# Memory attention and two Strassen MoE layers on one core: phi's relu and the gate's arithmetic move to POOL, and the order of the work is sought anew

## The chip, the cores and the metric

One Trainium2 chip, one of its cores. The time is that of one execution on the device, in microseconds (us); the median of several executions is given, and the range they span. Engines: PE is TensorE, DVE is VectorE, ACT is ScalarE, POOL is GpSimd, and SP issues nearly all DMAs.

## What is computed

```python
def _attn_ref(q, k, v, M_prev, z_prev, beta):      # B, H, S, D = 4, 8, 576, 64
    scores = scale * np.matmul(q, k.transpose(0, 1, 3, 2))   # causal mask, then softmax a
    local = np.matmul(a, v)
    def phi(x):
        return np.where(x > 0, x, np.exp(x) - 1.0) + 1.0
    q_p = phi(q)
    mem_ret = np.einsum('bhsd,bhde->bhse', q_p, M_prev)
    mem_norm = np.einsum('bhsd,bhd->bhs', q_p, z_prev)[..., None] + 1e-06
    mem_out = mem_ret / mem_norm
    g = 1.0 / (1.0 + np.exp(-beta))[None, :, None, None]
    return (g * mem_out + (1 - g) * local)

x = attn_out.transpose(0, 2, 1, 3).reshape(2304, 512)
h = x @ w_in; x = (h * tanh(softplus(h))) @ w_out      # first MoE layer, 512 -> 2048 -> 512
h = x @ w_in; x = (h * sigmoid(h)) @ w_out             # second MoE layer, the same sizes
```

## The kernel before, in words

The program is two stages that overlap a little. **Attention** works on 16 pairs of heads (4 batches x 4 pairs). For each pair, PE computes the scores in blocks of queries (steps `s40`, `s41`, `s3`, `s2`, `s1`, `s0`; L595 and L634), DVE evicts each block from PSUM with the mask added and the row's minimum taken (steps `r..`, L588, into a ring of four `sm` buffers), ACT takes the exponential with a row sum (steps `e..`, L615), PE transposes the probabilities (L486), ACT and DVE copy these out of PSUM (L476, L479), and PE multiplies by the values (L692). DVE scales the result into `xT` (L696).

Beside that runs phi of the queries, as a chain of small steps per pair on a 128x576 tile. Before, this chain is: `phu`, u = relu(nq) on ACT (L507); `phn`, e = nq - u on POOL (L505), which is min(nq, 0); `phe`, exp(e) on ACT (L506); `phf`, e + u on POOL (L508), which is phi(q); `phz` and `phy`, products with z on POOL (L509, L512); `phr`, the sum over a head on DVE (L513); `phg`, two small operations on POOL (L516, L517); `phd`, a reciprocal on DVE (L519); `phq`, a 128x8 product on DVE (L520); and the products that go into the probability tiles, on POOL (L534, L539). The softmax sums take the steps `za` (POOL, L641), `zd` (DVE, L643), `zg` and `n00` (POOL, L644 and L647).

The **gate** is computed once, on 128x8 tiles: exp(-beta) on ACT (L434), five operations on DVE (L437 to L441: 1 + exp, its reciprocal, 1 - g, a lower bound, a product), and five small copies on ACT (L446 to L452). Three steps of the first pair wait for it.

**The MoE layers** run on 32 visits (2 layers, 4 groups of the hidden width, 4 blocks of tokens), with 2 x 2 Strassen products in split single precision: L1000 to L1002 are a product's three matmuls, L1068 the second matmul of the layer, L1031 to L1041 the evictions and activations, L1089 the accumulation into `xT`. The weights arrive as raw 64-bit pairs and are decoded on DVE (L806 to L821; the first eight jobs begin on ACT, L804, and have their subtractions on POOL, L842 to L869, beside attention). L964 and L971 split the attention's result for the first products.

The order is not the program's text. Each step is put into a table with its engine, a duration, the steps it depends on and a due time; `plan` simulates the engines, takes on each free engine the ready step with the earliest latest start, and the instructions are issued in that order. A step's latest start is shifted by the numbers of `SHIFT`, a long table that a search has found. Each engine then runs its own list strictly in order, so an instruction whose input is late holds everything behind it on that engine. The functions `plan`, `pair_steps`, `gates`, `steps` and the `register` methods hold all that the change touches.

## Time and profile before

| | before |
|---|---|
| median of 3 runs | 951.5 us |
| lowest and highest run | 950.07 and 951.98 us |
| span of the profiled execution, first to last instruction | 949.0 us |
| PE busy | 921.2 us (97%) |
| DVE busy | 662.5 us (70%) |
| ACT busy | 498.9 us (53%) |
| POOL busy | 140.4 us (15%) |

Of the profiled execution the span is given; the three runs are timed by themselves and stand 1.1 to 3.0 us above it. The busy shares are means over both stages. Attention takes roughly the first 185 us of the span and all of POOL's work; from there on PE is the engine to look at. A row of groups reads: line, engine, operation, output<-inputs, shapes, count | busy us, mean ns of one | idle time of the engine before them and what ended it.

### The profile page before, as it was taken

The numbers are of one execution on the slowest core, as the hardware profiler recorded it, in microseconds if no ns is written. First come the engines' busy times: TensorE is split into PE (matmuls) and PEld (weight loads), VectorE is DVE, ScalarE is ACT, GpSimd is POOL, SyncE is SP. The second block draws the span as 40 slices with busy tenths as digits, with TensorE's granted clock in tenths as the row PEclk, the third lists the DMA queues.
The fourth block names the chain that finished last, engine by engine and source line by source line (L and its number), as shares of the span: only waits on it lengthen the run. The fifth ranks groups of instructions, "written<-read, shape, count | busy, mean of one in ns | idle before, by whom it ended". The sixth has DMA issues, their size and how long they took to land.

```text
span 949.0 us, 17264 instructions
## 1 busy us (share of the span) xinstructions
PE 921.2 (97%) x6544; PEld 813.1 (86%) x6544; DVE 662.5 (70%) x1504; ACT 498.9 (53%) x1172; POOL 140.4 (15%) x223
## 2 busy tenths in 40 slices
PE   4989999999999999999999999999999999999998
PEld 2656666799999999999999999998999888989986
DVE  4899899988984558665957889766647765754333
ACT  5998899876654243433433647554533442433330
POOL 5688798300000000000000000000000000000000
PEclk9999999999999999999999999999999999999999
DMA  6546563666647403850375535704550374024412
GB/s 209 149 158 194 165 199 121 213 261 235 221 150 250 156 1 98 274 156 1 117 253 197 221 119 198 278 23 162 189 177 10 108 265 145 1 93 147 157 54 99
DMA packets 60034, 147.72 MB, mean 156 GB/s; under 512 B 7600, under 2 KB 25136, under 8 KB 59952
## 3 DMA queue, kind: packets, MB, share of 16 engines
q1 hardware_dynamic: 59808, 146.30, 45.4%
q8 instruction: 51, 0.84, 0.4%
q10 hardware_dynamic: 144, 0.33, 0.1%
q14 instruction: 31, 0.25, 0.1%
HBM read 108.79 MB, written 37.81 MB: 154 GB/s over the span
## 4 chain that ended last, share of the span: by engine, by line
PE 85%; DVE 4%; ACT 3%; POOL 3%; issue 2%; DMA 2%; SPq 0%; DVEq 0%; POOLq 0%
PE acc L1068 42%; PE psX L1000 7%; PE psX L1001 7%; PE psX L1002 7%; PE psY L1000 4%; PE psY L1001 4%; PE psY L1002 4%; DVE sm L588 2%; PE psW L1001 2%; PE psW L1002 2%; PE psW L1000 2%; PE ps_t L692 2%; PE ps_s L595 2%; PE ps_t L486 1%; ACT Ph L615 1%
## 5 line engine op out<-in xcount | busy, mean ns | idle before, releaser
L1068 PE MATMUL acc<-g,w 128*128 128x320 f32 (+1 forms) x1152 | 218.3, 337 | 0.0
L1068 PE MATMUL acc<-w,g 128*128 128x512 f32 x864 | 214.4, 394 | 0.0
L1068 PEld LDWEIGHTS acc<-g,w 128*128 128x128 f32 x1152 | 183.8, 188 | 13.1
L1068 PEld LDWEIGHTS acc<-w,g 128*128 128x128 f32 x864 | 157.8, 188 | 30.5
L1031 ACT COPY vt<-psX 128x256 f32<-128x256 f32 (+1 forms) x192 | 75.2, 398 | 154.8 <-PE psX L1002 146.0
L1089 DVE TENSOR_TENSOR xT<-acc,xT 128x512 f32<-128x512 f32 (+1 forms) x126 | 77.2, 613 | 93.8 <-PE acc L1068 92.9
L1041 DVE TENSOR_TENSOR g<-vt,g 128x512 fp32r<-128x512 f32 (+1 forms) x128 | 94.1, 754 | 35.4 <-ACT g L1040 34.7
L1029 DVE TENSOR_TENSOR vt<-psY,vt 128x256 f32<-128x256 f32 (+1 forms) x128 | 57.9, 456 | 87.1 <-ACT vt L1031 46.2
L1040 ACT CAST g<-vt 128x512 fp32r<-128x512 f32 (+1 forms) x128 | 83.4, 672 | 31.5 <-PE acc L1068 30.1
L1000 PE MATMUL psX<-x,w 128*128 128x320 f32 (+1 forms) x256 | 75.8, 296 | 0.0
L1001 PE MATMUL psX<-x,w 128*128 128x320 f32 (+1 forms) x256 | 75.7, 296 | 0.0
L1002 PE MATMUL psX<-x,w 128*128 128x320 f32 (+1 forms) x256 | 75.6, 295 | 0.0
L595 PE MATMUL ps_s<-kT,qT 64*128 64x288 f32 (+3 forms) x320 | 66.8, 480 | 6.3 <-DMA kT<-in_kT_dram 4.6
L1037 ACT ACTIVATE vt<-vt 128x640 f32<-128x640 f32 (+1 forms) x64 | 43.8, 685 | 51.8 <-DVE vt L1029 51.5
L588 DVE CUSTOM_DVE_ANT_0 sm<-ps_s,mask 128x288 f32<-128x288 f32 (+3 forms) x128 | 56.9, 472 | 5.4 <-PE ps_s L595 3.1
L1035 ACT ACTIVATE vt<-vt 128x256 f32<-128x256 f32 (+1 forms) x64 | 28.5, 445 | 59.7 <-DVE vt L1029 59.7
L1036 ACT ACTIVATE vt<-psX 128x256 f32<-128x256 f32 (+1 forms) x64 | 26.0, 407 | 50.2 <-PE psX L1002 50.1
L1029 DVE TENSOR_TENSOR vt<-psW,vt 128x256 f32<-128x256 f32 (+1 forms) x64 | 29.1, 455 | 31.7 <-PE psW L1002 31.2
L1000 PEld LDWEIGHTS psX<-x,w 128*128 128x128 f32 x256 | 48.2, 188 | 2.0 <-issue 0.2
L1001 PEld LDWEIGHTS psX<-x,w 128*128 128x128 f32 x256 | 48.3, 189 | 1.7
L875 ACT CAST w<-val 128x512 fp32r<-128x512 f32 (+1 forms) x64 | 34.8, 567 | 26.5 <-DVE val L866 13.1
L1002 PEld LDWEIGHTS psX<-x,w 128*128 128x128 f32 x256 | 48.3, 188 | 0.0
(126 smaller groups left out, 2019.1 us busy)
## 6 DMA issues: line engine op xcount, KB each, us to landing
stg<-in_moe_w_in_dram SPq DMA_DIRECT2D x32, 512.0 KB, 5.6
stg<-in_moe_w_out_dram SPq DMA_DIRECT2D x32, 512.0 KB, 3.5
x<-sp SPq DMA_DIRECT2D x18, 640.0 KB, 4.2
x<-sp SPq DMA_DIRECT2D x18, 512.0 KB
sp<-x SPq DMA_DIRECT2D x12, 640.0 KB, 2.9
sp<-x SPq DMA_DIRECT2D x12, 512.0 KB, 4.1
nv<-in_v_dram SPq DMA_DIRECT2D x16, 320.0 KB, 4.3
x1T<-sp01T SPq DMA_DIRECT2D x8, 640.0 KB
```

What stands on the lines that cost most here:

```text
L588: nc.vector.tensor_tensor_reduce(out, ps, mask, -0.125, init, ALU.add, ALU.min, acc)
L595: nc.tensor.matmul(ps, lhsT=s["qT"][R[j], qcols(i)], rhs=s["kT"][R[j], k0 + cols.start:k0 + cols.stop], start=True, stop=True)
L1000: nc.tensor.matmul(o, lhsT=W(0, kc), rhs=X(0, kc), start=(n in (1, 2, 7) and kc == 0), stop=False, skip_group_check=True)
L1001: nc.tensor.matmul(o, lhsT=W(0, kc), rhs=X(1, kc), start=False, stop=False, skip_group_check=True)
L1002: nc.tensor.matmul(o, lhsT=W(1, kc), rhs=X(0, kc), start=False, stop=(kc == 1), skip_group_check=True)
L1029: nc.vector.tensor_tensor(o, self.bank[q, to], o, op=ALU.add)
L1031: f[f"s{n}"] = lambda n=n: nc.scalar.copy(val(*at[n]), self.bank[q, "X"])
L1037: f["m2"] = lambda: nc.scalar.activation(val(1), val(1), fn)
L1040: f[f"h{c}"] = lambda c=c: nc.scalar.copy(hi(c), val(c))
L1041: f[f"l{c}"] = lambda c=c: nc.vector.tensor_tensor(self.gt(q, c)[:, 1, :2 * tb], val(c), hi(c).bitcast(F32), op=ALU.subtract)
L1068: nc.tensor.matmul(y, lhsT=a, rhs=b, start=(c == 0 and k == 0), stop=(c == 1 and k == 5))
L1089: nc.vector.tensor_tensor(part, acc, part, op=ALU.add)
```

## The change

It makes five edits. (1) `phu` and `phn` become two independent one-input instructions on POOL: u = max(nq, 0) and e = min(nq, 0); ACT's relu goes. (2) Four of the five gate operations on DVE go to POOL, in two steps `one` and `rest` around the reciprocal `sig`, which stays on DVE. (3) The plan gains a `lock`: a DVE step in that set (`phq`, the weights' bit operations, the splits) is lengthened by what remains of a running POOL step, and a POOL step by what remains of such a DVE step. (4) Durations of the plan are set anew. (5) The table `SHIFT` is another one.

```diff
@@ plan @@
+        port = {"D": 0.0, "G": 0.0}
...
+                    if e == "D" and k in self.lock:
+                        d += max(0.0, port["G"] - now)
+                        port["D"] = now + d
+                    if e == "G":
+                        d += max(0.0, port["D"] - now)
+                        port["G"] = now + d
@@ pair_steps @@
-    E("phu", "A", 0.58, ["ldnq"])
-    E("phn", "G", 1.37, ["phu"])
+    E("phn", "G", 0.9, ["ldnq"])
     E("phe", "A", 0.58, ["phn"])
+    E("phu", "G", 0.9, ["ldnq"])
     E("phf", "G", 1.37, ["phe", "phu"])
@@ gates @@
+        def one():
+            nc.gpsimd.tensor_scalar(bt, bt, 1.0, None, op0=ALU.add)
+
         def sig():
-            nc.vector.tensor_scalar(bt, bt, 1.0, None, op0=ALU.add)
             nc.vector.reciprocal(self.g, bt)
-            nc.vector.tensor_scalar(self.g1, self.g, -1.0, 1.0, op0=ALU.mult, op1=ALU.add)
-            nc.vector.tensor_scalar(self.g1c, self.g1, 1e-20, None, op0=ALU.max)
-            nc.vector.tensor_tensor(self.btg, self.g1c, bt, op=ALU.mult)
+
+        def rest():
+            nc.gpsimd.tensor_scalar(self.g1, self.g, -1.0, 1.0, op0=ALU.mult, op1=ALU.add)
+            nc.gpsimd.tensor_scalar(self.g1c, self.g1, 1e-20, None, op0=ALU.max)
+            nc.gpsimd.tensor_tensor(self.btg, self.g1c, bt, op=ALU.mult)
@@ steps @@
-        f["phn"] = lambda: nc.gpsimd.tensor_tensor(self.get(p, "e"), s["nq"], s["u"], op=ALU.subtract)
+        f["phn"] = lambda: nc.gpsimd.tensor_scalar(self.get(p, "e"), s["nq"], 0.0, None, op0=ALU.min)
         f["phe"] = lambda: nc.scalar.activation(s["e"], s["e"], AF.Exp)
-        f["phu"] = lambda: nc.scalar.activation(self.get(p, "u"), s["nq"], AF.Relu)
+        f["phu"] = lambda: nc.gpsimd.tensor_scalar(self.get(p, "u"), s["nq"], 0.0, None, op0=ALU.max)
@@ register of the attention, of the weights, of the MoE @@
+                if n == "phq":
+                    m.lock.add((p, n))
-            slow = 0.05 if first else 0.0
-            for x, e, d, deps in (("ld", "S", 2.2, []), ("abs", "A", 0.53, ["ld"]) if first else ("abs", "D", 0.465, ["ld"]),
-                                  ("b0", "D", 0.465, ["abs"]), ("b1", "D", 0.465, ["b0"]), ("b2", "D", 0.735, ["b1"]),
-                                  ("b3", "D", 0.735, ["b2"])):
+            for x, e, d, deps in (("ld", "S", 2.2, []), ("abs", "A", 0.57, ["ld"]) if first else ("abs", "D", 0.335, ["ld"]),
+                                  ("b0", "D", 0.335, ["abs"]), ("b1", "D", 0.335, ["b0"]), ("b2", "D", 0.6, ["b1"]),
+                                  ("b3", "D", 0.6, ["b2"])):
+                if e == "D":
+                    m.lock.add(J(x))
-                d2 = lambda n: 0.25 + n / 480 if g == "G" else dve(n)
+                d2 = lambda n: 0.18 + n / 480 if g == "G" else dve(n)
+                m.lock.update(K(x) for x in ["l" + x for x in XOPS] + ["T1", "T2", "T3", "T4"])
-                act2 = lambda n, ps: (0.17 if ps else 0.212) + n / 1200
+                act2 = lambda n, ps: (0.067 if ps else 0.108) + n / 1200
@@ module @@
 def ps2(n):
-    return 0.126 + n / 960
+    return 0.07 + n / 960
 SHIFT = {
-    ('gate', 'exp'): -1546.35, ('gate', 'sig'): -1000.81, ('gate', 'spread'): -1110.7, ('a', 'ldkT'): -1506.04,
...
+    ('gate', 'exp'): -3248.83, ('gate', 'one'): 2030.47, ('gate', 'sig'): 4627.81, ('gate', 'rest'): 1314.36,
...
```

What that does to the lists is seen at three places. Lines shift by 8 to 17 in the changed file: its L600 is L588 of before, L627 is L615, L607 is L595, L517 to L521 are phi's L505 to L509.

The first is the start of DVE's list. L588 (L600) evicts scores; L437 to L441 and L448 are the gate. Before:

```order
L409 MEMSET warm 128x1
L437 TENSOR_SCALAR bt_102<-bt_102 128x8
L438 RECIPROCAL g<-bt_102 128x8
L439 TENSOR_SCALAR g_104<-g 128x8
L440 TENSOR_SCALAR g1c<-g_104 128x8
L441 TENSOR_TENSOR btg<-g1c,bt_102 128x8
L588 ISA sm,m_157<-ps_s,mask 128x288
L588 ISA m_157 128x1
```

Now:

```order
L417 MEMSET warm 128x1
L600 ISA sm,m_149<-ps_s,mask 128x288
L600 ISA m_149 128x1
L600 ISA sm,m_149<-ps_s,mask 128x288
L600 ISA m_149 128x1
L600 ISA sm,m_149<-ps_s,mask,m_149 128x288
L600 ISA m_149 128x1
L600 ISA sm,m_163<-ps_s,smask 128x64
L600 ISA m_163 128x1
L600 ISA sm,m_149<-ps_s,mask,m_149 128x288
L600 ISA m_149 128x1
L448 RECIPROCAL g<-bt_102 128x8
```

The first pair's five score evictions stood behind the whole gate; now they stand ahead of its one remaining DVE operation.

The second is the start of POOL's list, behind the constants. Before:

```order
L505 TENSOR_TENSOR e<-nq,u 128x576 x2
L508 TENSOR_TENSOR e<-e,u 128x576 x2
L509 TENSOR_TENSOR u<-e,z 128x512
L512 TENSOR_TENSOR u<-e,y 128x64
L509 TENSOR_TENSOR u<-e,z 128x512
```

Now:

```order
L519 TENSOR_SCALAR u<-nq 128x576 x2
L517 TENSOR_SCALAR e<-nq 128x576 x2
L445 TENSOR_SCALAR bt_102<-bt_102 128x8
L520 TENSOR_TENSOR e<-e,u 128x576
L451 TENSOR_SCALAR g_104<-g 128x8
L452 TENSOR_SCALAR g1c<-g_104 128x8
L453 TENSOR_TENSOR btg<-g1c,bt_102 128x8
L521 TENSOR_TENSOR u<-e,z 128x512
```

Both relus stand first, so the first pair's minimum is behind the relu of the second pair's queries, and the gate's sum is behind all four.

The third is POOL's list in the middle of attention. Before:

```order
L508 TENSOR_TENSOR e<-e,u 128x576
L505 TENSOR_TENSOR e<-nq,u 128x576
L509 TENSOR_TENSOR u<-e,z 128x512
L512 TENSOR_TENSOR u<-e,y 128x64
L516 TENSOR_SCALAR c<-c 128x9
L517 TENSOR_TENSOR c<-c,bt_108 128x9
L508 TENSOR_TENSOR e<-e,u 128x576
```

Now:

```order
L520 TENSOR_TENSOR e<-e,u 128x576
L517 TENSOR_SCALAR e<-nq 128x576
L521 TENSOR_TENSOR u<-e,z 128x512
L524 TENSOR_TENSOR u<-e,y 128x64
L520 TENSOR_TENSOR e<-e,u 128x576
L528 TENSOR_SCALAR c<-c 128x9
L529 TENSOR_TENSOR c<-c,bt_108 128x9
L519 TENSOR_SCALAR u<-nq 128x576
```

Each pair has one long POOL row more, the relu, and the plan puts it right behind the small operations on `c`.

Elsewhere the lists keep their make-up: up to its last attention instruction each list holds the same attention work but for the moved rows (ACT 16 relus fewer, POOL 20 instructions more), 18 MoE matmuls on PE as before, and the last 48 matmuls before the final group's own are in the same sequence.

## Rows read from the trace of the kernel before

**Rows 1.** Busy time by stretch: us, busy of each engine (instructions), granted clock, DMA, GB/s.

```profile
0.00:15.00 15.00, 2.78 (x14) 1.68 (x16) 4.03 (x11) 4.43 (x12) 6.60 (x14) 1.00 0.76 263
15.00:50.00 35.00, 32.23 (x335) 21.62 (x337) 30.72 (x121) 32.67 (x101) 23.92 (x41) 1.00 0.51 156
50.00:80.00 30.00, 26.40 (x309) 17.34 (x307) 26.22 (x88) 26.05 (x82) 26.46 (x40) 0.96 0.54 168
80.00:110.00 30.00, 29.03 (x318) 19.22 (x318) 26.87 (x96) 26.78 (x82) 22.88 (x37) 0.93 0.57 178
110.00:140.00 30.00, 28.35 (x359) 19.58 (x357) 28.66 (x99) 28.93 (x88) 27.91 (x41) 1.00 0.54 166
140.00:170.00 30.00, 28.28 (x348) 19.21 (x350) 28.54 (x107) 29.34 (x92) 25.65 (x43) 1.00 0.44 137
...
500.00:700.00 200.00, 200.00 (x1224) 183.91 (x1223) 150.72 (x285) 103.09 (x205) 0.00 (x0) 1.00 0.51 182
```

**Rows 2.** Waits of the whole span: engine, line, who ended it: us, times, longest.

```profile
DVE bt L437 <- ACT bt L434: 10.0, 1, 10.0
PE ps_s L634 <- DVE m L588: 7.8, 2, 7.6
```

**Rows 3.** Timeline of the first 24 us: start, length, instruction [idle before, what ended it].

```profile
4.65 2.29 PE L595 MATMUL ps_s<-kT,qT 64*128 64x288 f32 x8 [4.65 <-DMA kT<-in_kT_dram]
...
10.08 0.68 ACT L507 ACTIVATE u<-nq 128x576 f32<-128x576 f32 x1 [3.25 <-DMA nq<-in_q_dram]
...
13.98 0.46 DVE L588 CUSTOM_DVE_ANT_0 sm<-ps_s,mask 128x288 f32<-128x288 f32 x1
...
15.89 0.78 ACT L615 ACTIVATE Ph<-sm,m 128x576 f32<-128x576 f32 x1
...
17.33 0.62 DVE L588 CUSTOM_DVE_ANT_0 sm<-ps_s,mask 128x448 f32<-128x448 f32 x1 [1.33 <-PE ps_s L595]
...
19.56 1.12 PE L486 MATMUL ps_t<-ident,Ph 64*128 64x64 f32 x28
...
23.98 0.78 ACT L615 ACTIVATE Ph<-sm,m 128x576 f32<-128x576 f32 x1
```

**Rows 4.** Groups of POOL's instructions, in the first 186 us.

```profile
L505 POOL TENSOR_TENSOR e<-nq,u 128x576 f32<-128x576 f32 x16 | 22.8, 1422 | 6.5 <-ACT u L507 6.2
...
L647 POOL TENSOR_SCALAR P<-P,r,g1s 128x128 f32<-128x128 f32 x16 | 8.5, 529 | 4.0 <-DVE c L520 3.8 <-DVE r L643 0.3
...
L641 POOL TENSOR_SCALAR z<-z 128x9 f32<-128x9 f32 x16 | 3.9, 245 | 2.8 <-ACT Pl L615 1.7
...
L420 POOL TENSOR_SCALAR_AFFINE_SELECT smask<-smask 64x64 f32<-64x64 f32 x2 | 0.5, 234 | 0.1
...
L413 POOL TENSOR_SCALAR_AFFINE_SELECT mask<-mask 128x128 f32<-128x128 f32 x1 | 0.3, 292 | 0.1
```

**Rows 5.** ACT's group of relus, whole span.

```profile
L507 ACT ACTIVATE u<-nq 128x576 f32<-128x576 f32 x16 | 10.9, 678 | 7.6 <-DMA nq<-in_q_dram 7.2 <-DVE c L513 0.3
```

**Rows 6.** Chain that ended last: the relu's first and last piece after 15 us.

```profile
22.49 0.58 ACT u L507
...
137.37 0.23 ACT u L507
```

**Rows 7.** The same chain: one piece of phn.

```profile
162.26 1.38 POOL e L505
```

**Rows 8.** Line L520 alone: count, duration ns min/median/max, first and last start.

```profile
L520 DVE TENSOR_TENSOR c<-c,z x16: 101/298/1201, 24.3 to 174.8; 128x8 f32<-128x8 f32 x16
```

**Rows 9.** Line L814 alone, up to 186 us and after it.

```profile
L814 DVE TENSOR_SCALAR val<-val x8: 419/688/1328, 34.9 to 180.6; 128x512 f32<-128x512 f32 x8
...
L814 DVE TENSOR_SCALAR val<-val x56: 416/420/1521, 194.6 to 827.2; 128x512 f32<-128x512 f32 x56
```

**Rows 10.** Stretches of 5 us with a lower granted clock, columns as in rows 1.

```profile
75.00:80.00 5.00, 3.56 (x42) 2.51 (x43) 3.89 (x13) 3.18 (x10) 4.12 (x7) 0.75 0.74 239
...
105.00:110.00 5.00, 5.00 (x46) 3.09 (x45) 4.04 (x14) 4.21 (x13) 4.49 (x9) 0.68 0.90 278
```

More of the change, by code (lines that the diff above doesn't have):

```diff
@@ L50, in __init__ @@
         self.mode = {}
+        self.lock = set()
     def add(self, name, eng, dur, deps, fn, due, after=0.0, lag=0.0, cols=None):
@@ L452, in spread @@
                 nc.scalar.copy(self.g1s[r, :], gv[r, j, :])
-        return exp, sig, spread
+        return exp, one, sig, rest, spread
     def load(self, p, nm, queue=None):
@@ L511, in steps @@
             self.bt[b]["z"][:, h0:h0 + 2, :].unsqueeze(1).to_broadcast([P, 4, 2, D]), op=ALU.mult)
-        f["phy"] = lambda: nc.gpsimd.tensor_tensor(s["u"][:, 8], s["e"][:, 8], self.bt[b]["y"][:, hp], op=ALU.mult)
+        f["phy"] = lambda: nc.gpsimd.tensor_tensor(self.get(p, "u")[:, 8], s["e"][:, 8], self.bt[b]["y"][:, hp], op=ALU.mult)
         f["phr"] = lambda: nc.vector.tensor_reduce(out=self.get(p, "c"), in_=s["u"], axis=AX.X, op=ALU.add)
@@ L707, in register @@
         m.cap.update({"A." + r: t[4] for r, t in self.TILES.items()})
-        exp, sig, spread = self.gates()
+        exp, one, sig, rest, spread = self.gates()
         m.add(("gate", "exp"), "A", 0.2, [], exp, 25.0, 5.2)
-        m.add(("gate", "sig"), "D", 1.0, [("gate", "exp")], sig, 26.0)
-        m.add(("gate", "spread"), "A", 1.0, [("gate", "sig")], spread, 28.0)
+        m.add(("gate", "one"), "G", 0.2, [("gate", "exp")], one, 25.5)
+        m.add(("gate", "sig"), "D", 0.12, [("gate", "one")], sig, 26.0)
+        m.add(("gate", "rest"), "G", 0.6, [("gate", "sig")], rest, 27.0)
+        m.add(("gate", "spread"), "A", 0.75, [("gate", "rest")], spread, 28.0)
         for p in range(B * NP):
@@ L886, in register @@
             first = self.first(job)
-            slow = 0.05 if first else 0.0
-            for x, e, d, deps in (("ld", "S", 2.2, []), ("abs", "A", 0.53, ["ld"]) if first else ("abs", "D", 0.465, ["ld"]),
-                                  ("b0", "D", 0.465, ["abs"]), ("b1", "D", 0.465, ["b0"]), ("b2", "D", 0.735, ["b1"]),
-                                  ("b3", "D", 0.735, ["b2"])):
-                m.add(J(x), e, d + (slow if e == "D" else 0.0), [J(y) for y in deps], f[x], t,
+            for x, e, d, deps in (("ld", "S", 2.2, []), ("abs", "A", 0.57, ["ld"]) if first else ("abs", "D", 0.335, ["ld"]),
[3 more added lines that the diff above has]
+                    m.lock.add(J(x))
+                m.add(J(x), e, d, [J(y) for y in deps], f[x], t,
                       lag=1.6 if x == "ld" else 0.0, after=20.0 + 20.0 * n if first and x == "ld" else 0.0)
@@ L1250 @@
 SHIFT = {
-    ('gate', 'exp'): -1546.35, ('gate', 'sig'): -1000.81, ('gate', 'spread'): -1110.7, ('a', 'ldkT'): -1506.04,
[100 rows of a table removed]
+    ('gate', 'exp'): -3248.83, ('gate', 'one'): 2030.47, ('gate', 'sig'): 4627.81, ('gate', 'rest'): 1314.36,
+    ('gate', 'spread'): -895.27, ('a', 'ldkT'): -4376.92, ('ap', 0): -6657.88, ('a', 'ldqT'): -7408.66,
[93 rows of a table added]
 }
```

193 rows, old and new, of the table SHIFT are left out of this document.

## The prediction

> **What bounds the kernel now.** I read the busy time by stretch first [rows 1]. From the end of attention to the last matmul PE is busy in every microsecond: 200.00 of 200.00 us in the stretch that stands for them. Nothing on DVE, ACT or POOL can shorten that part, and the change removes no matmul. POOL works in attention alone. So the whole gain must come from the first 185 us, and the question is where PE waits there. In 15 to 170 us PE is busy 144.3 of 155 us, DVE 141.0, ACT 143.8 and POOL 126.8 (sums of five rows of [rows 1]): 93, 91, 93 and 82%. No engine is the bound by itself; work passes from one to the other, and each engine's list is strictly in order. In the first 15 us PE is busy for 2.78 us only.
>
> The waits say why [rows 2]. DVE waited 10.0 us for the gate's exponential, in front of L437, and PE waited 7.6 us in one piece for a score eviction. The timeline shows the rest [rows 3]. PE finished the first eight score matmuls at 6.94 (4.65 + 2.29). DVE evicted the first of them at 13.98 only, because the gate's five operations stood ahead of it in its list, and the gate's exponential stood on ACT behind a relu that waited for the second pair's queries, which landed just ahead of 10.08. The first softmax exponential ran at 15.89, the first transposes at 19.56.
>
> **The change, part by part.** The sum is made against the profiled span of 949.0 us; the median of the runs stands 2.5 us above it, and the same 2.5 are added at the end.
>
> *The gate and the head of the lists.* DVE's first evictions no longer have the gate ahead of them, so they can start when PE delivers, some 8 us before 13.98. That does not come through whole, since ACT's next piece is `phe` of the first pair, and on POOL the minimum that it needs is behind the second pair's relu. That relu starts when the queries land, at about 10.05. With 0.8 us for a one-input operation (below), relu ends at 10.85, the minimum at 11.65, `phe`, as wide as the relu and taken at its 0.68 [rows 5], at about 12.35, and the first softmax exponential starts there: 3.5 us before 15.89. The block that DVE evicts behind the gate's reciprocal follows POOL's `one`, about 12.6 with both minima, so it starts at 12.9 where it started at 17.33: 4.4 us. From the first exponential to the first transposes it took 3.67 us (19.56 - 15.89); now ACT's list has the second `phe`, the gate's five small copies and one narrow exponential more in between and waits less for DVE, an estimated 1.0 us more, so the transposes start at about 17.0, 2.5 us earlier. From there to the next pair's first exponential it took 4.42 us (23.98 - 19.56); two relus of 0.58 leave that stretch and one narrow exponential of about their half comes in, so this one starts at about 20.8, 3.2 us earlier. I take **-3.0 us**; the bounds are -2.5 and -4.4.
>
> *ACT's relus.* 16 instructions, 10.9 us of ACT [rows 5], of which two lie in the head. What they are worth is read from the chain that ended last: behind 15 us it holds five pieces of relu, four of 0.57 to 0.59 us and one of 0.23 [rows 6], together 2.54. The others lay beside work of other engines. I take **-2.5**; the bounds are 0, if the next wait is as long, and -8.1 (14 of them by 0.58), if ACT were the bound.
>
> *POOL's two for one.* A two-input pass over 576 elements takes 1422 ns [rows 4]. No one-input pass of that size is in the trace. The row nearest in its operands is the affine select: one input, no tensor of scalars, 234 ns at 64 columns and 292 at 128, so 0.91 ns an element and 0.70 us at 576. The row nearest in its name is L647, 529 ns at 128 columns, against 245 for 9 columns of L641: 2.39 ns an element and 1.60 us at 576; but it does two operations an element, with two scalars from tensors. Between 0.70 and 1.60 I take 0.8, close to the affine select, whose operands are those of relu and minimum. POOL then gets 16 x (2 x 0.8 - 1.42) = 2.9 us more, beside 28.2 idle in 15 to 170 (155 - 126.8). The chain holds three pieces of `phn`, 1.37 to 1.38 each [rows 7]; the relu can now run ahead whenever the queries are there, so at best each piece falls to 0.8 (-1.7), at worst both stand in it (+0.7). I take the dearer end, **+0.5**, since the plan puts the relu in the middle of POOL's list, behind `phg`, where it delays the next item.
>
> *The lock.* L520, an 8-column product, took 101 ns at its fastest, 298 in the median and 1201 at its slowest [rows 8]; L814 took 688 in the median beside attention and 420 behind it [rows 9]. DVE stands still then while POOL works: 16 x 0.197 and 8 x 0.268 are 5.3 us. The change does not remove that; it lets the plan see it. POOL is busy 82% of the time and gets more work, so I take **0**, between -2.6 (half avoided) and +0.5. The Trainium skill, "SBUF — State Buffer", section "Who interferes with whom", has a rule that speaks against this edit: the pair of ports that DVE and GpSimd share is held for a whole instruction by whichever began first, the other blocks, and ACT waits on no one. By that rule each relu taken from ACT adds to the time in which DVE can be blocked, and the sum would be 0.1 us worse (2.9 us more POOL on 140.4, of 5.3 us of stalls); the rows of L520 bear it out that the wait reaches a whole POOL instruction.
>
> *The new order.* In MoE PE has no idle time to win. A late eviction or weight would cost PE its whole length; I take 0, since DVE and ACT are busy 150.7 and 103.1 of 200 us there [rows 1]. The tail keeps its sequence of matmuls: 0.
>
> The sum is -3.0 - 2.5 + 0.5 = -5.0, a span of 944.0 and a time of **946.5 us**. A measurement of this kernel can tell about 0.2%, 1.9 us, from no change.
>
> **The rivals.** *More than that.* PE's idle time in 15 to 170 us is 10.7 us (155 - 144.3), and the granted clock was 0.75 in 75 to 80 us, where PE was busy for 3.56 of 5 only, and 0.68 in 105 to 110 [rows 10]: parts of these stretches ran at 1.2 GHz and the rest at 2.4, which lost 5 x 0.25 + 5 x 0.32 = 2.9 us. An order that is fitted better could win half of these 13.6 beside the head: 951.5 - 3.0 - 6.8 = 941.7. For it: the plan of before priced DVE's weight operations without the wait that the rows show. Against: four engines above 80% leave little to reorder.
>
> *No change.* The head's 3 us are lost again at the next late transfer or full ring, since all lists behind it are new: 951.5, within 1.9. Then the edit about the lock would not do what it says either: the order is planned around the lock, but the chip's POOL and DVE meet elsewhere, and L520's median stays at 298.
>
> *POOL becomes the bound, slower.* If relu and minimum cost L647's rate, 1.60 us each, POOL gets 16 x 1.78 = 28.5 us more, 24.9 of them in 14 pairs behind 15 us, where it had 28.2 idle. It would be 98% busy, which its waits for ACT and DVE do not allow. If 10 us of these waits stay, attention grows by about 7; the head gains 1.9 only (two operations of 0.8 us more ahead of `phe`); 951.5 + 7 - 1.9 = 956.6. It decides from about 1.36 us an operation, where 18 us are added. The Trainium skill, "GPSIMD Engine Reference", section "Elementwise — side-by-side cycle accounting", gives 2.6 cycles an element for two inputs and 1.03 for a light body; by the second figure and the 1.2 GHz that it states, 576 elements are an estimated 0.49 us beside the start, and the sum would be 1 us better than mine; by the first, 1.25 us, it would come near this rival.
>
> *A stall in MoE, slower.* One eviction or weight load late by 3 to 6 us on a PE without slack takes the gain back: about 951 to 955. Against: before, PE did not wait there at all.
>
> **How the numbers follow.** The forecast has 0.55 (times of 943 to 949.5), the better order 0.12 (937 to 943), no change 0.16, POOL as the bound 0.12, a stall in MoE 0.05. Faster by over 0.2% are the first two, 0.67; the same 0.16; slower 0.17. The range must leave out no more than 0.2: 940 to 954 holds the forecast, no change, half of the better order and a third of the slower cases, 0.83.
>
> **What would show it.** Right: the first eviction on DVE starts before 7 us and the first transposes near 17; no relu on ACT; the two one-input rows at 0.7 to 0.9 us; POOL's busy time near 144 us (140.4 + 2.9 + four small rows of the gate); PE without idle time from the end of attention on; PE reaching the first second-layer matmuls 4 to 6 us earlier. Wrong: one-input rows above 1.3 us with POOL over 95% busy, a new long wait of PE or a lower clock between 20 and 180 us, or any idle time of PE in MoE.

## The result and the profile after

The changed kernel takes 957.8 us in the median (955.9 to 959.6), the kernel before 951.7 in the runs beside it: the ratio is 1.0066, with a 95% interval of 1.0046 to 1.0085. It is slower by 6 us, where 946.5 was forecast, and the time lies outside the range. The time is that of the rival "POOL becomes the bound, slower" (956.6), in part by luck, as told below.

The page of the changed kernel:

```profile
span 955.5 us, 17182 instructions
...
PE 923.2 (97%) x6544; PEld 813.3 (85%) x6544; DVE 652.9 (68%) x1500; ACT 494.5 (52%) x1156; POOL 170.1 (18%) x243
...
PE 87%; POOL 6%; DVE 3%; issue 1%; DMA 1%; SPq 1%; ACT 1%; DVEq 0%; POOLq 0%; ACTq 0%
```

POOL's busy time was 140.4 us and is 170.1; the forecast said 144. The last row is the chain that ended last, by engine: POOL has 6% of it, before 3%. Of the 6.5 us that the span is longer, PE's busy time has 2.0 (921.2 to 923.2) and PE's idle time 4.5. All of it lies in attention: POOL's last row that goes into the probability tiles starts at 183.39 us, before at 176.50.

Busy time by stretch, columns as in [rows 1]:

```profile
0.00:15.00 15.00, 5.60 (x20) 3.79 (x20) 1.92 (x11) 3.32 (x7) 9.01 (x16) 1.00 0.66 220
15.00:170.00 155.00, 138.75 (x1602) 92.90 (x1602) 136.88 (x485) 132.69 (x414) 146.10 (x206) 0.98 0.54 163
110.00:140.00 30.00, 26.44 (x295) 17.00 (x297) 26.20 (x92) 25.09 (x76) 29.05 (x42) 0.94 0.54 176
140.00:170.00 30.00, 28.30 (x336) 19.28 (x332) 27.41 (x90) 24.85 (x77) 28.52 (x39) 0.95 0.52 149
500.00:700.00 200.00, 200.00 (x1244) 185.00 (x1243) 151.05 (x293) 103.75 (x211) 0.00 (x0) 1.00 0.51 183
```

In 15 to 170 us POOL is busy 146.1 of 155 us (94%; before 126.8, [rows 1]), and the other three engines all do less there than before: PE 138.8 (144.3), DVE 136.9 (141.0), ACT 132.7 (143.8). One engine rose and the others wait for it, so that less of attention is done in this stretch. PE's idle time fell by 2.8 us in the first 15 (12.2 to 9.4) and rose by 5.5 in the next 155 (10.7 to 16.2). MoE is as full as before.

POOL's groups, first 200 us; the first and the last answer to L505 and L647 of [rows 4]:

```profile
L517 POOL TENSOR_SCALAR e<-nq 128x576 f32<-128x576 f32 x16 | 27.5, 1723 | 0.3
L519 POOL TENSOR_SCALAR u<-nq 128x576 f32<-128x576 f32 x16 | 27.2, 1700 | 5.2 <-DMA nq<-in_q_dram 5.2
L520 POOL TENSOR_TENSOR e<-e,u 128x576 f32<-128x576 f32 x16 | 22.9, 1434 | 1.3 <-ACT e L518 1.2
...
L659 POOL TENSOR_SCALAR P<-P,r,g1s 128x128 f32<-128x128 f32 x16 | 7.2, 448 | 2.6 <-DVE r L655 1.4 <-DVE c L532 1.2
```

The minimum and the relu take 1.72 and 1.70 us each, not 0.8. A pass with one input and a constant is dearer here than the sum of two tensors of the same size (L520, 1.43). 54.7 us stand where 22.8 stood: 31.9 more, with 29.7 net on POOL.

Waits of the first 200 us, columns as in [rows 2]:

```profile
ACT e L518 <- POOL e L517: 14.6, 9, 8.0
...
PEld ps_t L577 <- POOL rx L656: 8.9, 9, 1.6
...
DVE g L448 <- POOL bt L445: 6.2, 1, 6.2
PE ps_s L646 <- DVE m L600: 6.2, 3, 5.0
```

The two waits of [rows 2] had DVE behind ACT and PE behind DVE. Now ACT's exponential waits for POOL's minimum, PE's transposes of the sums wait for POOL's `rx`, DVE's reciprocal for POOL's gate sum. PE's wait for DVE's score evictions is still there, 6.2 us in place of 7.8.

The head, columns as in [rows 3]:

```profile
6.42 1.66 POOL L519 TENSOR_SCALAR u<-nq 128x576 f32<-128x576 f32 x1 [3.20 <-DMA nq<-in_q_dram]
7.15 0.46 DVE L600 CUSTOM_DVE_ANT_0 sm<-ps_s,mask 128x288 f32<-128x288 f32 x1 [6.30 <-PE ps_s L607]
...
10.08 1.64 POOL L519 TENSOR_SCALAR u<-nq 128x576 f32<-128x576 f32 x1 [2.00 <-DMA nq<-in_q_dram]
11.69 3.26 POOL L517 TENSOR_SCALAR e<-nq 128x576 f32<-128x576 f32 x2
13.37 0.68 ACT L518 ACTIVATE e<-e 128x576 f32<-128x576 f32 x1 [8.00 <-POOL e L517]
13.96 0.76 ACT L627 ACTIVATE Ph<-sm,m 128x576 f32<-128x576 f32 x1
...
15.20 0.20 DVE L448 RECIPROCAL g<-bt 128x8 f32<-128x8 f32 x1 [6.18 <-POOL bt L445]
...
19.41 1.76 PE L498 MATMUL ps_t<-ident,Ph 64*128 64x64 f32 x28 [0.85 <-ACT Ph L627]
```

DVE's first eviction starts at 7.15, where it was 13.98. The chain behind it is the one that the prediction followed, relu at 10.08, minimum, `phe`, first softmax exponential, but in steps of 1.65 us in place of 0.8: the exponential is at 13.96 where 12.35 was forecast, and the first transposes are at 19.41, 0.15 us ahead of before.

### The profile page after: what moved, and what is told of

It is laid out like the page before. It is cut to its first block, busy times and chain, and to the rows that moved or that the text cites. A ratio compares the mean times of both kernels' runs of the same rounds, so it can differ in the third digit from the quotient of the medians.

```text
span 955.5 us, 17182 instructions
## 1 busy us (share of the span) xinstructions
PE 923.2 (97%) x6544; PEld 813.3 (85%) x6544; DVE 652.9 (68%) x1500; ACT 494.5 (52%) x1156; POOL 170.1 (18%) x243
## 4 chain that ended last, share of the span: by engine, by line
PE 87%; POOL 6%; DVE 3%; issue 1%; DMA 1%; SPq 1%; ACT 1%; DVEq 0%; POOLq 0%; ACTq 0%
PE acc L1085 42%; PE psX L1017 7%; PE psX L1018 7%; PE psX L1019 7%; PE psY L1017 4%; PE psY L1018 4%; PE psY L1019 4%; PE ps_t L704 3%; PE ps_s L607 2%; PE psW L1017 2%; PE psW L1018 2%; PE psW L1019 2%; PE ps_t L498 2%; POOL e L517 1%; DVE sm L600 1%
## 5 line engine op out<-in xcount | busy, mean ns | idle before, releaser
L1085 PE MATMUL acc<-g,w 128*128 128x320 f32 (+1 forms) x1152 | 213.2, 337 | 0.0
L1057 ACT CAST g<-vt 128x640 fp32r<-128x640 f32 (+1 forms) x128 | 82.3, 673 | 92.3 <-PE acc L1085 91.1
L1017 PE MATMUL psX<-x,w 128*128 128x256 f32 (+1 forms) x256 | 75.7, 296 | 0.0
L1018 PE MATMUL psX<-x,w 128*128 128x256 f32 (+1 forms) x256 | 75.7, 296 | 0.0
L1019 PE MATMUL psX<-x,w 128*128 128x256 f32 (+1 forms) x256 | 75.6, 295 | 0.0
L607 PE MATMUL ps_s<-kT,qT 64*128 64x288 f32 (+3 forms) x320 | 65.4, 483 | 5.1 <-DMA kT<-in_kT_dram 4.7
L600 DVE CUSTOM_DVE_ANT_0 sm<-ps_s,mask 128x288 f32<-128x288 f32 (+3 forms) x128 | 56.3, 470 | 8.2 <-PE ps_s L607 7.5
L1053 ACT ACTIVATE vt<-psX 128x320 f32<-128x320 f32 (+1 forms) x64 | 26.3, 411 | 53.6 <-PE psX L1019 53.6
L627 ACT ACTIVATE Ph<-sm,m 128x576 f32<-128x576 f32 (+1 forms) x64 | 46.1, 721 | 4.4 <-DVE m L600 4.0
L837 DVE SCALAR_TENSOR_TENSOR val<-stg,val 128x512 uint32<-128x512 uint32 x64 | 46.9, 737 | 0.5
```

The source lines that it names most:

```text
L600: nc.vector.tensor_tensor_reduce(out, ps, mask, -0.125, init, ALU.add, ALU.min, acc)
L607: nc.tensor.matmul(ps, lhsT=s["qT"][R[j], qcols(i)], rhs=s["kT"][R[j], k0 + cols.start:k0 + cols.stop], start=True, stop=True)
L837: nc.vector.scalar_tensor_tensor(out=cu, in0=hi, scalar=0xC0000000, in1=cu, op0=ALU.bitwise_and, op1=ALU.bitwise_or)
L1017: nc.tensor.matmul(o, lhsT=W(0, kc), rhs=X(0, kc), start=(n in (1, 2, 7) and kc == 0), stop=False, skip_group_check=True)
L1018: nc.tensor.matmul(o, lhsT=W(0, kc), rhs=X(1, kc), start=False, stop=False, skip_group_check=True)
L1019: nc.tensor.matmul(o, lhsT=W(1, kc), rhs=X(0, kc), start=False, stop=(kc == 1), skip_group_check=True)
```

## The experiments

Three causes had to be told apart: the price of the two passes (theory P), the new order (O), and DVE's waits for the port that it shares with POOL (L). All ratios are to the kernel before, run beside each. Kernels of different groups ran on different chips and are compared by these ratios; one thousandth of the ratio is 0.95 us.

### Both passes made cheap

```diff
-        f["phn"] = lambda: nc.gpsimd.tensor_scalar(self.get(p, "e"), s["nq"], 0.0, None, op0=ALU.min)
+        f["phn"] = lambda: nc.gpsimd.affine_select(out=self.get(p, "e"), in_=s["nq"], pattern=[[0, 9], [0, D]], compare_op=ALU.is_ge, fill=0.0, base=1, channel_multiplier=0)
```

and the same for `phu` into u. The select keeps every element, so both passes copy the queries: this kernel leaves out the minimum and the maximum and shows the time alone.

> The changed kernel with both one-input passes (relu and minimum, 1.64 to 1.72 us each in its profile) replaced by an affine select that keeps every element, so u and e are plain copies of the queries; the plan and the order of all five lists are those of the changed kernel, row for row. From the affine select's rows (234 ns at 64 columns, 292 at 128) each should take 0.7 us, 16 x 2 x 1.0 = 32 us less of POOL. Theory P, the price of the pass made POOL the bound of attention: POOL's busy time falls from 170 to about 138, and the time from 957.8 to 944 to 949, below the kernel before. Theory O, the new order is worse by itself: the time stays above 953 although POOL is relieved. Theory L, DVE's waits for the shared port are the cause: the time falls only as far as the means of DVE's 8-column product (499 ns) and of the weights' bit operations (684 to 1135 ns) fall.

Measured: 940.7 us, ratio 0.9896 (0.9874 to 0.9918). POOL's and DVE's groups of this kernel:

```profile
L517 POOL TENSOR_SCALAR_AFFINE_SELECT e<-nq 128x576 f32<-128x576 f32 x16 | 12.6, 788 | 0.3
...
L532 DVE TENSOR_TENSOR c<-c,z 128x8 f32<-128x8 f32 x16 | 5.3, 332 | 0.0
```

its first transposes and one stretch of it:

```profile
16.74 1.75 PE L498 MATMUL ps_t<-ident,Ph 64*128 64x64 f32 x28 [0.21 <-ACT Ph L627]
...
15.00:170.00 155.00, 148.45 (x1779) 101.00 (x1778) 145.38 (x523) 140.45 (x445) 131.62 (x222) 1.00 0.56 172
```

With nothing changed but the price of these 32 passes, the change is 1% faster, not 0.7% slower: 16 us for the 29.0 that POOL no longer works (170.1 - 141.1). PE gets 148.5 busy us into the stretch, at a granted clock of 1.00 (2.4 GHz); over the whole span its busy time falls by 2.4 us only (923.2 to 920.8), so the clock is a small part. Theory P is shown, though the time came below the 944 to 949 expected of it, and O falls: the order as such costs nothing. L is a small part too. L532 takes 2.7 us less than in the changed kernel ((499 - 332) x 16), and the weights' bit operations beside attention (L830 to L837, 29 instructions) hardly change: 25.1 us in the changed kernel, 24.8 here.

### One of the two passes made cheap

The diff above for `phn` alone.

> The changed kernel with the minimum alone made cheap (an affine select that copies the queries into e, so e is not the minimum), the relu as it is on POOL: 0.79 + 1.72 = 2.5 us a pair of these two passes, where the changed kernel has 3.4, the run with both cheap 1.6 and the run with all edits but the relu 1.42. All five lists are otherwise row for row the changed kernel's. If the time grows in step with POOL's work (940.7 at 1.6, 957.8 at 3.4): 949 to 950. If POOL's slack hides the first part, as the prediction's slower rival has it (it decides from about 1.36 us an operation, 2.72 a pair): 941 to 945. POOL's busy time near 156.

Measured: 947.8 us, ratio 0.9971 (0.996 to 0.9982). Groups:

```profile
L519 POOL TENSOR_SCALAR u<-nq 128x576 f32<-128x576 f32 x16 | 27.3, 1705 | 6.5 <-DMA nq<-in_q_dram 5.2 <-DVE c L525 1.3
...
L517 POOL TENSOR_SCALAR_AFFINE_SELECT e<-nq 128x576 f32<-128x576 f32 x16 | 13.1, 820 | 0.3
...
L532 DVE TENSOR_TENSOR c<-c,z 128x8 f32<-128x8 f32 x16 | 6.6, 412 | 0.0
```

The time came between the two expected ranges, nearer to that of a cost in step with POOL's work; neither half of the added work is free. With the two passes at 1.6, 2.5 and 3.4 us a pair, the ratio is 0.9896, 0.9971 and 1.0066: the first 14.4 us of POOL (141.1 to 155.5) cost 0.0075, some 7.1 us, the next 14.6 cost 0.0095, some 9. Between the last two the ratio passes 1 at an estimated 2.8 us a pair, 1.4 an operation.

### The two passes on the old order

The kernel before with the two lambdas of the change, its plan left alone (the new order is not in it).

```diff
-        f["phn"] = lambda: nc.gpsimd.tensor_tensor(self.get(p, "e"), s["nq"], s["u"], op=ALU.subtract)
+        f["phn"] = lambda: nc.gpsimd.tensor_scalar(self.get(p, "e"), s["nq"], 0.0, None, op0=ALU.min)
-        f["phu"] = lambda: nc.scalar.activation(self.get(p, "u"), s["nq"], AF.Relu)
+        f["phu"] = lambda: nc.gpsimd.tensor_scalar(self.get(p, "u"), s["nq"], 0.0, None, op0=ALU.max)
```

> The kernel before with the first edit alone, in its own order: relu as a one-input pass on POOL at the place in the sequence where it stood on ACT, and the minimum as another; no other edit, the plan untouched. POOL gets 16 x (1.65 + 1.7 - 1.42) = 31 us more, ACT 16 x 0.58 = 9.3 less. Theory P: slower than before by 6 us or more, 957 to 970, with POOL over 95% busy in attention. Theory O: within 2 us of the kernel before, or faster, as ACT is relieved.

Measured: 971.0 us, ratio 1.0215 (1.0186 to 1.0244), 1 us above the expected range; POOL is busy 138.0 of 155 us (89%) in 15 to 170, not over 95%. The longest of its waits, of the first 200 us, and a row of its page:

```profile
PEld ps_t L565 <- POOL rx L644: 11.6, 9, 3.1
...
PE 931.6 (96%) x6544; PEld 818.1 (85%) x6544; DVE 661.5 (68%) x1504; ACT 492.8 (51%) x1156; POOL 169.5 (18%) x239
```

The passes cost some 20 us on the old order (0.0215 by 951.5) and 15 on the new one (957.8 against 943.0, below). The difference is not in the waits. Of the spans' 18.7 us (967.7 against 949.0) PE's busy time has 10.4 (931.6 against 921.2), with a granted clock of 0.94 in 15 to 170 us, part of it at 1.2 GHz; on the new order it has 4.9 of 14.1 (923.2 against 918.3), at 0.98. That leaves 8.3 and 9.2 us that PE waits longer, much the same on both orders.

### All edits but the relu, and the relu alone back

First only the relu goes back to ACT, the minimum stays a one-input pass:

```diff
-        f["phu"] = lambda: nc.gpsimd.tensor_scalar(self.get(p, "u"), s["nq"], 0.0, None, op0=ALU.max)
+        f["phu"] = lambda: nc.scalar.activation(self.get(p, "u"), s["nq"], AF.Relu)
```

> The changed kernel with the relu alone back on ACT, the minimum still on POOL, in the same planned order: each relu stands on ACT where it stood in the sequence of the plan. POOL loses 16 x 1.7 = 27 us, ACT gets 16 x 0.58 = 9.3 us. Theory P: 945 to 951, since POOL's busy time is then about 143 us, what it was before the change. Theory O: above 953. Since the order was not made for it, ACT's relus may stand badly; a time between 949 and 953 would not tell the two apart, and the first run decides.

Measured: 944.2 us, ratio 0.9932 (0.991 to 0.9953), just below theory P's range. Then the minimum goes back as well, so that both operations are those of before, in the new order:

```diff
-        f["phn"] = lambda: nc.gpsimd.tensor_scalar(self.get(p, "e"), s["nq"], 0.0, None, op0=ALU.min)
+        f["phn"] = lambda: nc.gpsimd.tensor_tensor(self.get(p, "e"), s["nq"], s["u"], op=ALU.subtract)
```

> The changed kernel with its first edit undone in the operations alone: the relu on ACT again, the minimum as the two-input difference on POOL, and every list in the changed kernel's order with the relu at the plan's place. So it is the edits on the gate, the lock, the durations and the table alone. My theory (the price of two slow POOL passes is all that is wrong with the change): 941 to 945, a little better than the run with the relu alone on ACT (944.2), since each of 16 two-input differences is 0.28 us cheaper than the one-input minimum (4.5 us of POOL), but the minimum waits for ACT's relu again. Rival: the two-input difference has to wait for ACT where the one-input minimum did not, so 944 to 950. Second rival: the edits without the relu bring nothing, 950 to 953.

Measured: 943.0 us, ratio 0.9907 (0.989 to 0.9923), as expected. Its first transposes, and by stretch:

```profile
17.27 1.76 PE L498 MATMUL ps_t<-ident,Ph 64*128 64x64 f32 x28 [0.88 <-ACT Ph L627]
...
0.00:15.00 15.00, 6.73 (x30) 4.62 (x31) 3.68 (x20) 6.27 (x13) 7.27 (x18) 1.00 0.75 249
15.00:170.00 155.00, 146.16 (x1770) 98.73 (x1770) 144.12 (x518) 146.14 (x458) 131.41 (x209) 1.00 0.56 172
```

Edits 2 to 5 alone are worth 0.9%, more than the whole forecast. PE's idle time falls by 3.9 us in the first 15 (12.2 to 8.3) and by 1.9 in the next 155 (10.7 to 8.8), and the granted clock there is 1.00 where the five rows of [rows 1] have 0.96 and 0.93 among them. The changed kernel differs from this one in the two operations and is 14.7 us slower.

### The head

Onto that kernel (all edits but the relu), the head of before was put back:

```diff
-        for k in self.plan():
+        late = {(1, "phu"): [("gate", "exp")], (0, "phn"): [("gate", "one"), ("gate", "sig"), ("gate", "rest")]}
+        moved = [x for v in late.values() for x in v]
+        for k in [x for k in self.plan() if k not in moved for x in [k] + late.get(k, [])]:
...
-            nc.gpsimd.tensor_scalar(bt, bt, 1.0, None, op0=ALU.add)
+            nc.vector.tensor_scalar(bt, bt, 1.0, None, op0=ALU.add)
```

and the same engine for the other three gate operations.

> The run with all edits but the relu (943.0), with the head of the kernel before put back: the gate's exponential behind the second pair's relu on ACT, and all five gate operations on DVE, ahead of the first score eviction. Everything behind is in the same order. My theory (the prediction's first step, -3.0 us for the gate off the head of DVE's list, between -2.5 and -4.4): 945.5 to 947.5, the first eviction back at 13.5 to 14 us and the first transposes 2 to 3 us later than 17.3. Rival (the order of the 150 us behind it carries the gain, and a later head is caught up, since ACT and POOL have slack there): 943 to 944.5.

Measured: 948.0 us, ratio 0.9966 (0.9952 to 0.998), above the 945.5 to 947.5 expected; by the ratios 5.6 us more than without this head (0.9966 - 0.9907). Its timeline on DVE, and PE's first transposes:

```profile
11.04 1.38 DVE L447 TENSOR_SCALAR bt<-bt 128x8 f32<-128x8 f32 x1 [10.17 <-ACT bt L444]
12.45 0.20 DVE L450 RECIPROCAL g<-bt 128x8 f32<-128x8 f32 x1
12.69 1.08 DVE L453 TENSOR_SCALAR g<-g 128x8 f32<-128x8 f32 x1
13.80 0.17 DVE L454 TENSOR_SCALAR g1c<-g 128x8 f32<-128x8 f32 x1
14.01 1.11 DVE L455 TENSOR_TENSOR btg<-g1c,bt 128x8 f32<-128x8 f32 x1
15.04 0.44 DVE L602 CUSTOM_DVE_ANT_0 sm<-ps_s,mask 128x288 f32<-128x288 f32 x1
...
21.24 1.76 PE L500 MATMUL ps_t<-ident,Ph 64*128 64x64 f32 x28
```

The first eviction is 1.1 us later than in the kernel before (13.98), the first transposes are at 21.24 where before had 19.56 and the kernel without this head has 17.27. Of the 4.0 us between the last two, 1.7 are this head being worse than the old one, and the old one's own share is 2.3. The 5.6 us at the end show that what the head loses is not caught up behind it.

In the other direction, the second pair's phi was moved behind the gate and the first pair's phi:

```diff
-        for k in self.plan():
+        late = {("gate", "rest"): [(1, "phu")], (0, "phy"): [(1, "phn"), (1, "phe")]}
+        moved = [x for v in late.values() for x in v]
+        for k in [x for k in self.plan() if k not in moved for x in [k] + late.get(k, [])]:
```

> The run with all edits but the relu, and one thing moved: at the head, the relu of the second pair goes behind the gate's last POOL operations and its minimum and exponential behind the first pair's y-product, so that the first pair's phi and the gate no longer wait for the second pair's queries (which land just ahead of 10.05 us). My theory (the head's 2.5 us in the prediction were limited by that wait): the first softmax exponential starts at 8.5 to 10 us, the first transposes at 13.5 to 15, and the time is 2 to 3 us below the same kernel without the move. Rival: the next pair, whose phi is now later, takes it back, or the fitted order behind it does not fit any more: within 1 us of the same kernel, or slower by up to 4.

Measured: 941.75 us, ratio 0.9895 (0.9878 to 0.9912); beside it on the same chip the kernel without the move had 943.0, and the two sets of times don't overlap (941.55 to 942.4, and 942.46 to 943.23).

```profile
8.95 0.76 ACT L629 ACTIVATE Ph<-sm,m 128x576 f32<-128x576 f32 x1
```

The first exponential starts 2.9 us earlier than at 11.80, the transposes 1.6 earlier (15.67), the end 1.3: the exponential as expected, the transposes 0.7 later than that, the end half of it. This is the fastest of these kernels that leaves nothing out, 10 us ahead of the kernel before and 16 of the changed one.

### Both on ACT

On the kernel with all edits but the relu:

```diff
-        f["phn"] = lambda: nc.gpsimd.tensor_tensor(self.get(p, "e"), s["nq"], s["u"], op=ALU.subtract)
+        f["phn"] = lambda: nc.scalar.activation(self.get(p, "e"), s["nq"], AF.Relu, scale=-1.0)
-        f["phe"] = lambda: nc.scalar.activation(s["e"], s["e"], AF.Exp)
+        f["phe"] = lambda: nc.scalar.activation(s["e"], s["e"], AF.Exp, scale=-1.0)
```

> The run with all edits but the relu (943.0), with the minimum moved the other way: ACT computes e = relu(-nq) and then exp(-e), which is the same function, and POOL loses 16 two-input passes of 1.42 us (its busy time falls to about 118). ACT gets 16 relus more, some 9.5 to 11 us, 8 of them in 14 pairs behind 15 us, where it was busy 146 of 155. Theory A (POOL is what phi waits for): 940 to 943, as in the run with cheap POOL passes. Theory B (ACT, at 94%, becomes the bound, as POOL did in the changed kernel): 944 to 951, ACT above 97% in 15 to 170 us, and DVE and PE waiting for its exponentials and copies.

Measured: 947.7 us, ratio 0.9969 (0.9959 to 0.9979).

```profile
15.00:170.00 155.00, 143.06 (x1708) 95.50 (x1708) 142.66 (x512) 151.07 (x465) 108.07 (x189) 1.00 0.54 165
```

ACT is busy 151.1 of 155 us (97%), POOL 70%: theory B. Here POOL waits for ACT (18.2 us for phi's exponential, 7 times). 8.3 us more of ACT (507.7 against 499.4) cost some 6 by the ratios, although POOL was relieved of 23 (118.2 against 141.2). So it is not POOL alone: whichever of the two gets more work, the others wait for it.

### What a POOL pass costs

The kernel before, with unused POOL instructions ahead of its list, two rounds of one line each:

```diff
+        for _ in range(2):
+            nc.gpsimd.tensor_scalar(pr, a, 0.0, None, op0=ALU.max)
...
+            nc.gpsimd.affine_select(out=pr, in_=a, pattern=[[-1, NQ]], compare_op=ALU.is_ge, fill=0.0, base=1000, channel_multiplier=1)
```

> The kernel before with two rounds of POOL instructions on 576 columns (one of 288) added at the start, writing a tile that nothing reads; its own time is not the question (POOL's list starts some 25 us later, so attention ends later). Question: what sets the 1.70 us of relu and minimum on POOL in the changed kernel. Theory P1 (any tensor-scalar instruction runs at one slow rate there, whatever the operation): maximum, minimum, sum and product with one constant all take 1.60 to 1.75 us, the 288-column one about half of it plus the start (0.85 to 0.95), and a tensor copy and the affine select 0.7 to 0.9. Theory P2 (maximum and minimum alone are slow): sum and product take 0.7 to 1.2 us. Theory P3 (waiting for DVE or DMA traffic stretched them, the instruction is cheap by itself): all of them below 1.2 us here at the start, where DVE is nearly idle. Two-input sums and products, for comparison: 1.3 to 1.45 us by all three.

Its groups; L420 to L423 are maximum, minimum, sum and product with one constant, L424 maximum then product, L425 product then sum, L426 the maximum on 288 columns, L427 the sum of a tensor with itself, L429 a copy:

```profile
L424 POOL TENSOR_SCALAR pr<-mask 128x576 f32<-128x576 f32 x2 | 4.3, 2142 | 0.2
...
L420 POOL TENSOR_SCALAR pr<-mask 128x576 f32<-128x576 f32 x2 | 3.3, 1648 | 0.2
...
L427 POOL TENSOR_TENSOR pr<-mask 128x576 f32<-128x576 f32 x2 | 2.3, 1144 | 0.2
L426 POOL TENSOR_SCALAR pr<-mask 128x288 f32<-128x288 f32 x2 | 1.9, 927 | 0.2
L425 POOL TENSOR_SCALAR pr<-mask 128x576 f32<-128x576 f32 x2 | 1.4, 680 | 0.2
L430 POOL TENSOR_SCALAR_AFFINE_SELECT pr<-mask 128x576 f32<-128x576 f32 x2 | 1.3, 666 | 0.2
```

Theory P1: 1.65 to 1.66 us whatever the one operation is, 0.93 for half the columns, so about 2.5 ns an element ((1648 - 927) / 288) and 0.2 us of start. It is the instruction's own time (P3 falls): in the changed kernel, beside other work, the same row is 1.70. The surprise is L425. A second probe looked for other forms with its short time:

```diff
+            nc.gpsimd.tensor_relu(pr, a)
+            nc.gpsimd.tensor_scalar(pr, a, 1.0, 0.0, op0=ALU.mult, op1=ALU.max)
...
+            nc.gpsimd.tensor_scalar(pr, a, 1.0, 1.0, op0=ALU.add, op1=ALU.mult)
```

> As the first probe: the kernel before with two rounds of POOL instructions on 576 columns ahead of its own list, writing a tile that nothing reads; its own time is not the question. The first probe had one operation with a constant at 1.65 us for maximum, minimum, sum and product alike, maximum then product at 2.14, but product then sum at 0.68. This one asks which forms share the short time: the relu instruction; product then maximum, product then minimum, sum then maximum, maximum then sum, maximum twice; product twice, sum twice, sum then product, product then subtraction, product then nothing; and product then sum again. Theory F1 (product then sum is one form with a path of its own, all others are slow): it alone takes 0.68, the two-operation forms 2.1, product then nothing 1.65, and the relu instruction 1.65 too. Theory F2 (two arithmetic operations are fast, and maximum and minimum are slow): product twice and sum twice near 0.7, those with a maximum or minimum near 2.1. Theory F3 (a first product makes it fast): product then maximum and product then minimum near 0.7, in which case relu and minimum can have the price that the prediction took.

Lines L419 to L430 in the order of that text (the relu instruction is L419, product then maximum L420):

```profile
L426 POOL TENSOR_SCALAR pr<-mask 128x576 f32<-128x576 f32 x2 | 4.3, 2152 | 0.2
...
L420 POOL TENSOR_SCALAR pr<-mask 128x576 f32<-128x576 f32 x2 | 4.3, 2146 | 0.2
...
L419 POOL TENSOR_SCALAR pr<-mask 128x576 f32<-128x576 f32 x2 | 3.3, 1656 | 0.2
...
L425 POOL TENSOR_SCALAR pr<-mask 128x576 f32<-128x576 f32 x2 | 1.4, 675 | 0.2
L427 POOL TENSOR_SCALAR pr<-mask 128x576 f32<-128x576 f32 x2 | 1.3, 672 | 0.2
```

Three forms are short: product then sum (L430, 0.68), product twice (L425) and sum then product (L427). Sum twice (L426), product then subtraction (L428) and every two-operation form with a maximum or minimum take 2.14 to 2.15, one operation alone 1.65, product then nothing (L429) too. None of the three theories fits: F1 is nearest. No form tried gives a maximum or minimum at the price that the prediction took.

### Plans made anew

Two kernels let the planner make the lists again with a table that was not searched for them: before with the gate's edit alone, and the changed kernel with its plan's price of both passes at 1.6.

```diff
-    E("phn", "G", 0.9, ["ldnq"])
+    E("phn", "G", 1.6, ["ldnq"])
...
-    E("phu", "G", 0.9, ["ldnq"])
+    E("phu", "G", 1.6, ["ldnq"])
```

> The changed kernel with the plan's price of the minimum and of the relu at 1.6 instead of 0.9 us, and all lists planned anew with the same table of shifts. Theory A (the plan was misled by a price that the chip does not have, and knows better with the right one): 950 to 955, three us or more below the changed kernel. Theory B (the cost is POOL's work itself; a plan with a table that was searched for other durations only gets worse, as in the run with the gate's edit alone): 957 to 970.

> The kernel before with the second edit alone: four of the gate's five DVE operations on POOL in two steps, the old durations and the old table of shifts, the lists planned anew. DVE's first score evictions then stand ahead of the gate's reciprocal. Theory P: the head's gain is there without the pass's price, the first eviction at about 7 us instead of 13.98, the first transposes 2 to 3 us earlier, and the time 947 to 950. Rival: the head's gain does not reach the end of attention, because a later wait takes it (a transfer, a full ring): 951 to 953.

Measured: 965.2 us for the price of 1.6 (ratio 1.0144, 1.0125 to 1.0163; theory B), 962.4 for the gate alone (1.0126, 1.0102 to 1.015; its diff is edit 2 of the change), outside both of its ranges. In the second, one stretch:

```profile
15.00:170.00 155.00, 141.49 (x1624) 94.81 (x1624) 137.72 (x490) 138.80 (x429) 123.99 (x193) 0.96 0.52 164
```

Its head did what was expected: the first eviction starts at 6.84 us and the first transposes at 16.17, 3.4 us ahead of before. Behind it PE is busy 2.8 us less in this stretch than before, at a granted clock of 0.96, with POOL at 80%. In both runs a table that was searched for other steps lost time: a better price cost 7 us against the changed kernel, and steps taken off DVE cost 12 against the one before. So planning anew can't separate edits 3, 4 and 5, and what the lock, the durations or the table bring by themselves stays open.

## Why the prediction was wrong, point by point

**POOL's two for one, +0.5: the step that failed, in the price of 0.8 us an operation.** "Between 0.70 and 1.60 I take 0.8, close to the affine select, whose operands are those of relu and minimum." The chip gives 1.70 and 1.72, above the upper bound. Likeness of operands was the wrong guide: the affine select itself costs 0.79, as the forecast took it, but a tensor-scalar instruction with a maximum or a minimum does not run like it. The row nearest in its name, L647, gave 1.60 and was put aside; that it came so near is luck in part, since it does two operations, and two operations with constants took 0.67 or 2.14 in the probes. The 29.0 us of POOL between the two prices cost 16.2 (1.0066 - 0.9896, by 951.5), on top of the term's 0.5. By itself that would have given 962.7 (946.5 + 16.2); the new order, below, won 4.9 more than was forecast.

**The rival.** "POOL becomes the bound" said 28.5 us more of POOL (29.7 came) and 956.6 (957.8 came). The place is right, the sum is right by luck: it put the cost at 7 us and the gain at 1.9, and the runs show 16.2 and 9.9 (941.6 against 951.5). POOL is 94% busy, not 98%, and the cost begins with the first microseconds added, not at 1.36 us an operation; 1.4 is only where it has used up the gain. The chance of 0.12 was too low, since it hung on one price between two rows and the forecast on the other.

**The head, -3.0: right as a place, undone by the price.** Relu, minimum and `phe` stood in the order and on the queries' landing as described. With less work on POOL the transposes are at 16.95 (minimum on POOL, relu on ACT) and 16.74 (both copies), where 17.0 was forecast; in the changed kernel they are at 19.41. The 20.8 us for the next pair's exponential is 20.6 by its own terms, and the bounds of the step allow for that. Against the kernel with all edits but the relu the old head's share is 2.3 us there, and the run with the old head put back shows that it is not caught up; the run with the second pair moved away shows 1.3 us that the change left there.

**ACT's relus, -2.5: not settled.** The kernel with both cheap passes and the one with all edits but the relu have the same POOL time (141.1 and 141.2 us) and differ by ACT's relus (and by the minimum's wait for them): 0.9896 against 0.9907, 1 us, with intervals that hold 0 and 2.5.

**The lock, 0: right while the passes are cheap, too low in the changed kernel.** The prediction counted L520's waits by its median; the mean is 444 ns. With both passes cheap its successor L532 takes 332, 1.8 us less for 16, but the weights' bit operations beside attention take 24.8 us where they took 22.5, so the two together gain nothing (0.5 us more). In the changed kernel both are dearer than before, by 0.9 and 2.6 us (25.1), beyond the bound of +0.5:

```profile
L520 DVE TENSOR_TENSOR c<-c,z 128x8 f32<-128x8 f32 x16 | 7.1, 444 | 0.0
...
L532 DVE TENSOR_TENSOR c<-c,z 128x8 f32<-128x8 f32 x16 | 8.0, 499 | 0.0
```

With the same lists, POOL's busy time of 141.1, 155.5 and 170.1 us goes with 332, 412 and 499 ns. The rule of the Trainium skill in "SBUF — State Buffer", section "Who interferes with whom", that the shared pair of ports is held for a whole instruction, speaks in the right direction, and these three numbers agree. But between cheap and dear passes that is 2.7 us over 16 instructions, and 0.3 on the weights, beside 16 in all.

**The new order, 0: too low.** With the passes at the forecast's price the change gives 0.9896, 941.6 us: the case "More than that" (941.7), for which there was 0.12. In the two kernels that have the new order and none of the slow passes PE waits 1.9 and 4.2 us less from 15 to 170 us, and the granted clock is 1.00 there. The forecast left the 2.9 us of lower clock [rows 10] as they were, but they belong to the profiled execution: the executions of before at a mean granted clock of 1.000 have a median span 0.4 to 0.9 us below that of all of them, chip by chip, so the clock can be little of the 4.9. **MoE, 0:** right; 200.00 of 200.00 us.

## What to carry to other kernels

When an operation moves to another engine, its price there decides, and neither the number of its inputs nor the name of the instruction gives it: on POOL the same instruction took 0.67 to 2.15 us by its operations. Where a rival hangs on such a price, time the very form first, with an unused instruction ahead of a list, or take the dear end. In this kernel, with four engines above 80%, POOL's slack was not free: a microsecond added to it cost 0.5 to 0.6 us from the start. Planning anew could not cost a single edit of an order that was searched for given durations; pinned lists with one operation changed did.

## What the runs showed of the hardware that was not expected

On POOL, over 576 columns of 32-bit floats: one operation with a constant 1.65 us, two 2.14, but product then sum, sum then product and product twice 0.67 to 0.68, as a copy or an affine select. The Trainium skill, "GPSIMD Engine Reference", section "Elementwise — side-by-side cycle accounting", has 1.03 cycles an element for a light body; an estimated 0.49 us for 576 elements at its 1.2 GHz, with 0.2 us of start, agrees with these short forms (0.67). A single relu takes 2.4 times as long, and for it the measurement decides. A sum of two different tensors took 1.43 us and a sum of a tensor with itself 1.14.

Small DVE operations can take longer for POOL's sake than for their own: in the run with the old head three of the gate's 128x8 instructions took 1.38, 1.08 and 1.11 us, others of their size 0.17 to 0.20. The three ended at 12.42, 13.77 and 15.12 us, each 0.02 to 0.04 behind the end of the POOL pass that ran beside it (1.40 us from 10.98, 1.40 from 12.35, 1.27 from 13.82).
